# Attention and experts on one core: the experts' operands from split 32-bit floats to scaled pairs of 16-bit floats

## The chip, the cores and the metric

The kernel runs on one core of one Trainium2 chip. Its engines are PE (TensorE: matrix products, with weight loads listed as PEld), DVE (VectorE), ACT (ScalarE), POOL (GpSimd) and SP (SyncE, which here issues DMAs). Each works through its own queue in order. The metric is the device time of one execution in microseconds (us), the median of several runs.

## The reference

Attention with pooled queries for 8 batches of 8 heads, and then a mixture of 8 experts in which each token goes to one:

```python
q_pool = q.reshape(B, H, S // 2, 2, D).mean(axis=3)            # B=8 H=8 S=1152 D=64
scores = np.matmul(q_pool, k.transpose(0, 1, 3, 2)) / np.sqrt(D)
attn = softmax(scores)                                          # + 1e-9 in the sum
x = np.matmul(attn, v)  ->  rows of 512, N = 4608
logits = x @ w_gate
e_idx = np.argmax(logits, axis=1)
for e in range(8):
    h = np.maximum(x[mask] @ w1[e], 0.0)                        # w1: 512 x 1024
    ye = h @ w2[e]                                              # w2: 1024 x 512
    out[mask] = gate_w[mask, None] * eom[mask, e, None] * ye
```

## The kernel before

All products are exact to about 32-bit floats: a 32-bit operand is split into a high part that TensorE takes at speed and a low part with the rest, and a product is the sum of three: high by high, high by low, low by high.

**Attention** works on 32 pairs of heads, 18 steps each (one step is one head and 128 keys, 576 steps in all). In each step PE makes the scores of step s (two matmuls of 512 columns, L466), 1.5 products for row maxima two thirds of a pair ahead (L388, read by DVE at L389), and the product with v of the step six before (L495 to L497, 12 small matmuls a chunk, each with its weight load). ACT takes the exponential (L442), and for five of the 18 steps (PLP) a second one (L444) from which DVE subtracts; in the others POOL makes the low part (L450). The splitting of the next pairs' q, k and v is spread over the steps by tables (PREP0, PREPF, PREPE, PREP; three slots a step, counted from SLEAD steps before the start); their copies to the places where PE reads them are DMAs on SP. BURST says how many chunks of the product with v fall into which step. After each batch a router finds every token's expert, writes its row of x with its gate to the scratch tensor xrows (513 wide) and scatters its number into lists by expert.

**Experts** work on tiles of 256 tokens of one expert. Before attention ends, 256 tokens of the expert that leads by then are already gathered (tile -1); then come 18 dynamic tiles of 256 (two halves of 128) and 3 tiles of 128 ("one half", list 'S'). A tile's weights (4 MB) are loaded into raw1 and raw2, which are double, unless the expert is the same. For tile t, tile_ and head write out the order of PE, DVE and ACT by hand: layer one in four groups g (l1m makes the products into PSUM, l1e reads them out: ACT copies the half that comes from x's low part, DVE adds, ACT takes the relu, DVE the low part hl), with the split of w2 (split2) between them; then the split of the next tile's w1 (split1), layer two for the first 128 tokens (l2), the transposes of the next tile's x (xt: PE transposes, ACT copies the high part, DVE subtracts), layer two for the other half. y is scaled by the token's gate (xg column 512) and scattered to the output. A half tile's layer two uses plain 32-bit floats. The split parts are of type F32R: W1 and W2 exist once, x is double. A matmul of F32R brings its weight load with it. POOL has the gathers and scatters: after the last router 5 scatters, then the gathers of numbers (L839) and of rows (L850).

The products of layer one stand as follows, x holding its high part in columns 0 to w and its low part in w to 2w, W1[0] being the high part of w1:

```python
for c in range(4):
    for l in (0, 1) if c == 0 else (1, 0):
        n = w if l else 2 * w
        nc.tensor.matmul(hp[:, f, 0:n], lhsT=W1[l][g][:, c, fs], rhs=d['x'][:, c, 0:n], ...)
```

## Time and profile before

| | us |
|---|---|
| median of 3 runs | 1444.39 (1443.15 to 1447.83) |
| the profiled execution | 1445.07 |
| its span, first to last instruction | 1443.4 |
| PE busy | 1403.0 (97%) |
| DVE busy | 1095.0 (76%) |
| ACT busy | 976.2 (68%) |
| POOL busy | 1008.2 (70%) |

The trace comes from one execution, and its times are counted from the span's start. "Busy" is time in which at least one instruction of an engine runs; matmuls overlap, so PE's pace is read from the distance between the starts of successive matmuls, not from the length of one. [...] In the rows, five busy times stand in the order PE, PEld, DVE, ACT, POOL, each with its number of instructions; a tile name is the program's, `out<-in`, followed by shapes; a bracket at the end of a row is the time that the engine stood idle before it and what it waited for.

### The profile page before, as it was taken

What the parts mean: (1) busy time and instruction counts of PE and PEld (TensorE: products, weight loads), DVE (VectorE), ACT (ScalarE), POOL (GpSimd) and SP (SyncE); (2) the same over time, 40 slices, a digit from 0 to 9 for tenths busy, and PEclk for the clock granted to TensorE, in tenths of its full rate; (3) what the DMA queues carried; (4) which work ended last, traced back from release to release, by engine and by line L of the source; (5) the groups of instructions that cost most, each with busy time, mean ns of one, the idle gap of its engine ahead of it and who ended that gap; (6) DMA issues with size and microseconds to landing.
All of it is one profiled execution on the core that took longest, in us unless ns stands there. A gap on an engine that the chain in (4) does not pass through costs nothing. (4 is left out here: it accounts for less than half of the span.)

```text
span 1443.4 us, 40161 instructions
## 1 busy us (share of the span) xinstructions
PE 1403.0 (97%) x16056; PEld 1037.8 (72%) x16056; DVE 1095.0 (76%) x2404; ACT 976.2 (68%) x1769; POOL 1008.2 (70%) x1036
## 2 busy tenths in 40 slices
PE   7999999999999999999999999989999999999996
PEld 4566667666666666666666666778888888888874
DVE  6677878887887887787787887578787877778652
ACT  6687777777777877877776776746565655656542
POOL 6888999899899989989989998872323333323200
PEclk8999999999999999999999999999999999999999
DMA  4345344443553463354354432639546666363650
GB/s 155 106 131 157 114 122 131 132 122 99 141 145 89 124 166 94 96 164 125 88 145 117 138 116 62 234 106 360 173 154 232 222 235 232 122 219 98 230 188 8
DMA packets 92048, 212.57 MB, mean 147 GB/s; under 512 B 13357, under 2 KB 28925, under 8 KB 91855
## 3 DMA queue, kind: packets, MB, share of 16 engines
q1 hardware_dynamic: 81262, 188.35, 42.7%
q0 software_dynamic: 9152, 20.85, 4.2%
q8 instruction: 128, 2.10, 0.6%
q10 hardware_dynamic: 1440, 0.74, 0.2%
q14 instruction: 66, 0.53, 0.1%
HBM read 164.23 MB, written 23.02 MB: 130 GB/s over the span
## 5 line engine op out<-in xcount | busy, mean ns | idle before, releaser
L389 DVE TENSOR_REDUCE pm<-mp 128x1 f32<-128x384 f32 x864 | 447.5, 549 | 75.3 <-PE mp L388 68.9
L442 ACT ACTIVATE p<-sps 128x512 f32<-128x512 f32 x576 | 343.0, 596 | 207.6 <-PE sps L466 163.7
L450 POOL TENSOR_TENSOR pl<-p 128x512 f16<-128x512 f32 x414 | 423.2, 1040 | 61.2 <-ACT p L442 58.1
L388 PE MATMUL mp<-ka,qa 128*128 128x384 f16 x960 | 297.9, 327 | 3.0 <-DVE pm L389 2.4
L495 PE MATMUL av<-vt,p 128*128 128x65 f16 x2304 | 252.7, 193 | 0.3 <-DVE xb L514 0.3
L496 PE MATMUL av<-vt,p 128*128 128x64 f16 x2304 | 252.4, 194 | 0.0
L497 PE MATMUL av<-vt,pl 128*128 128x65 f16 x2304 | 252.2, 192 | 0.1
L388 PE MATMUL mp<-kb,qb 66*128 66x384 f16 x768 | 251.1, 327 | 0.0
L495 PEld LDWEIGHTS <-p 128*128 128x128 bf16 x2304 | 215.0, 97 | 27.1 <-DVE xb L514 1.0
L1021 PE MATMUL hps<-x,w1h 128*128 128x512 f32 (+1 forms) x704 | 228.7, 386 | 5.0 <-DVE x L1004 4.4
L496 PEld LDWEIGHTS <-p 128*128 128x128 bf16 x2304 | 213.2, 97 | 25.9 <-issue 0.2
L466 PE MATMUL sps<-qb,kb 69*128 69x512 f16 x576 | 219.4, 381 | 0.7 <-DMA qb<-mr 0.7
L466 PE MATMUL sps<-qa,ka 128*128 128x512 f16 x576 | 219.0, 380 | 0.0
L497 PEld LDWEIGHTS <-pl 128*128 128x128 f16 x2304 | 212.5, 98 | 0.3 <-POOL pl L450 0.3
L1021 PE MATMUL hps<-x,w1l 128*128 128x256 f32 (+1 forms) x704 | 164.7, 275 | 0.0
L1030 ACT COPY hs<-hps 128x512 f32<-128x512 f32 (+1 forms) x88 | 49.1, 558 | 170.4 <-PE hps L1021 162.6
L388 PEld LDWEIGHTS <-qa 128*128 128x128 f16 x960 | 94.4, 98 | 86.0 <-issue 1.3
L447 DVE TENSOR_TENSOR pl<-sps,p 128x512 f16<-128x512 f32 x162 | 111.2, 686 | 43.0 <-ACT sps L444 39.3
L1021 PEld LDWEIGHTS hps<-x,w1l 128*128 128x128 f32 x704 | 131.2, 189 | 12.9
L1021 PEld LDWEIGHTS hps<-x,w1h 128*128 128x128 f32 x704 | 121.8, 188 | 21.0 <-DVE x L1004 5.1
L839 POOL DMA_INDIRECT ids<-idscr,riD x36 | 43.8, 1215 | 131.7 <-DMA out_dram<-y,ids 121.0
L388 PEld LDWEIGHTS <-qb 66*128 66x128 f16 x768 | 75.3, 98 | 72.8 <-issue 8.4
(265 smaller groups left out, 3157.7 us busy)
## 6 DMA issues: line engine op xcount, KB each, us to landing
raw1b<-in_w_dram SPq DMA_DIRECT2D x24, 1024.0 KB
raw2b<-in_w_dram SPq DMA_DIRECT2D x24, 1024.0 KB
raw1a<-in_w_dram SPq DMA_DIRECT2D x22, 1024.0 KB
raw2a<-in_w_dram SPq DMA_DIRECT2D x22, 1024.0 KB
vp<-in_vL_dram SPq DMA_DIRECT2D x32, 576.0 KB
kpf<-in_kT_dram SPq DMA_DIRECT2D x31, 576.0 KB
qp<-in_qT_dram SPq DMA_DIRECT2D x31, 576.0 KB
ka<-xk SPq DMA_DIRECT2D x120, 144.0 KB
```

The costliest lines, as they stand in the source:

```text
L388: nc.tensor.matmul(mp, lhsT=l, rhs=r, start=j == 0, stop=j == len(ops) - 1)
L389: nc.vector.tensor_reduce(out=pm[:, i:i + 1], in_=mp, axis=AX.X, op=ALU.max)
L442: e_ = nc.scalar.activation(out=p32, in_=x, func=AF.Exp, scale=1.0 / 16)
L447: nc.vector.tensor_tensor(out=pl, in0=x, in1=ph, op=ALU.subtract)
L450: nc.gpsimd.tensor_tensor(out=pl, in0=p32, in1=ph, op=ALU.subtract)
L466: nc.tensor.matmul(x, lhsT=l, rhs=r, start=j == 0, stop=j == 1)
L495: nc.tensor.matmul(av_[:, qb, 0:65], lhsT=hi, rhs=vt[:, h, c, 0:65], start=c == 0 and qb == 0, stop=False)
L496: nc.tensor.matmul(av_[:, qb, 0:64], lhsT=hi, rhs=vt[:, h, c, 66:130], start=False, stop=False)
L497: nc.tensor.matmul(av_[:, qb, 0:65], lhsT=lo, rhs=vt[:, h, c, 0:65], start=False, stop=e and qb == 3 and h == 0)
L839: i = nc.gpsimd.indirect_dma_start(out=ids, out_offset=None, in_=self.idscr, in_offset=bass.IndirectOffsetOnAxis(ap=idx[:, j:j + 1], axis= ...
L1021: nc.tensor.matmul(hp[:, f, 0:n], lhsT=W1[l][g][:, c, fs], rhs=d['x'][:, c, 0:n], start=c == 0 and l == 0, stop=c == 3 and l == 0)
L1030: nc.scalar.copy(out=hs, in_=hp[:, :, w:2 * w])
```

## The change

Every operand of the experts becomes a pair of 16-bit floats (F16) instead of a pair of F32R. So that 16 bits hold them, weights and x are scaled by powers of two.

- *Scales of the weights.* During attention all 16 weight matrices are read once in 64 pieces of 512 KB (wst, on SP's queue), and ACT sums the magnitudes of each piece along its columns (wmag; from step 12 on, the loads six steps ahead of the sums, at steps 3, 11, 19, 23 and 35 of each 36). Near the end of attention wscale adds these over the rows (one matmul of 64 columns) and makes wt: for each expert one over the scale for w1 and w2, the scale of w1, and the product of both scales. pick takes a tile's expert out of wt with a one-hot product.
- *Scale of x.* rowscale takes each token's largest magnitude (DVE, over 512 columns), rounds it to a power of two, takes the reciprocal, lets ACT scale the gathered row in place, and puts what undoes all scales into gp, by which y is now scaled.
- *Splits.* cutw: ACT writes the high part, scaled, and DVE the low part in one pass. For tile -1's w1 ACT first scales in place, and POOL subtracts; its last w2 split goes from POOL to DVE.
- *Two sets* of split W1 and W2, one for tiles of either parity.
- *Layer one* is three products of w columns, each with its own weight load, into the same w columns; so nothing has to be added afterwards, and a group takes half the PSUM (three buffers instead of two). Relu and hl read PSUM.
- *Order.* xs (scl and rowscale for the next tile) stands after group 1; a half tile's next x is transposed ahead of layer two; in head xs stands ahead of split1, and two of the four split1 behind xt.
- y has 12 buffers instead of 4. The tables of attention (PREP, PREPE, BURST, PLP, TAIL, FWD, SLEAD) have new numbers; PREPE, PREP0 and PREPF are the same relative to the steps.

The rest of the experts (the part under tc.If) gets the same, and does not run with these inputs.

```diff
-FWD = 12
...
+FWD = 15
...
-BURST = {0: 1, 1: 2, 2: 1, 4: 1, 5: 1, 6: 1, 7: 2, 9: 1, 10: 1, 12: 1, 13: 2, 14: 1, 15: 3, 16: 1}
-PLP = (2, 8, 10, 11, 14)
+BURST = {0: 2, 1: 2, 4: 1, 5: 1, 6: 1, 7: 2, 10: 1, 11: 1, 12: 1, 13: 2, 14: 1, 15: 2, 16: 2}
+PLP = (3, 9, 10, 11, 13)
+WS0, WSP, WSL = 18, (3, 11, 19, 23, 35), 6
-TAIL = (10, 13, 15)
+TAIL = (10, 11, 15)
-SLEAD = 36
+SLEAD = 37
...
+        wm, wadd = moe.wmag(ld, lambda: sq.tile([128, S], F16, name="kjunk")), []
+        wsc = moe.wscale(psum, free)
...
+                if s >= WS0 - WSL and (s + WSL) % 36 in WSP:
+                    x = next(wm, None)
+                    if x is not None:
+                        wadd.append(x)
+                if wadd and s >= WS0 and s % 36 in WSP:
+                    wadd.pop(0)()
+                if WS0 + 36 * (64 // len(WSP) + 1) <= s < 18 * NP:
+                    next(wsc, None)
+                if moe.P1 and s == 18 * NP - 10:
+                    moe.rowscale(-1, 2, keep['px1'])
...
+                        nc.sync.dma_start(out=wst, in_=self.w1v[e, :, q])
...
+                    def add(wst=wst, i=i):
+                        nc.scalar.activation(out=junk()[:, 0:1024], in_=wst, func=AF.Abs, scale=2.0 ** -17, accum_out=self.keep['ws'][:, i:i + 1])
+                    yield add
...
+    def wscale(self, psum, free):
+        nc, k = self.tc.nc, self.keep
+        V, wt = nc.vector, k['wt']
+        g, gk = psum(True)
+        nc.tensor.matmul(g[:, 0:64], lhsT=k['ones'], rhs=k['ws'].bitcast(BF16)[:, 1::2], start=True, stop=True)
...
+        V.tensor_scalar(out=wt[:, 2:4].rearrange("p m e -> p (m e)"), in0=x, scalar1=2.0 ** -100, scalar2=2.0 ** 3, op0=ALU.max, op1=ALU.mult)
...
+        V.reciprocal(out=wt[:, 0:2], in_=wt[:, 2:4])
...
+    def pick(self, t, oh, s4, tm):
+        V, wt = self.tc.nc.vector, self.keep['wt']
+        V.tensor_tensor(out=tm, in0=wt, in1=oh.unsqueeze(1).broadcast_to([128, 4, 8]), op=ALU.mult)
+        V.tensor_reduce(out=s4, in_=tm, axis=AX.X, op=ALU.add)
+        self.T[t]['s'] = s4
+
+    def rowscale(self, t, h, px):
+        nc, d = self.tc.nc, self.T[t]
+        V = nc.vector
+        mx, sx, gp = px[:, 0:h], px[:, 2:2 + h], px[:, 4:4 + h]
+        for j in range(h):
+            V.tensor_reduce(out=mx[:, j:j + 1], in_=d['xg'][j][:, 0:512], axis=AX.X, op=ALU.max, apply_absolute_value=True)
+        V.tensor_scalar(out=mx.bitcast(U32), in0=mx.bitcast(U32), scalar1=0x7F800000, scalar2=None, op0=ALU.bitwise_and)
+        V.tensor_scalar(out=mx, in0=mx, scalar1=2.0 ** -100, scalar2=2.0, op0=ALU.max, op1=ALU.mult)
+        V.reciprocal(out=sx, in_=mx)
+        for j in range(h):
+            nc.scalar.activation(out=d['xg'][j][:, 0:512], in_=d['xg'][j][:, 0:512], func=AF.Copy, scale=sx[:, j:j + 1])
+            V.scalar_tensor_tensor(out=gp[:, j:j + 1], in0=d['xg'][j][:, 512:513], scalar=d['s'][:, h + 1:h + 2], in1=mx[:, j:j + 1], op0=ALU.mult, op1=ALU.mult)
+        d['gp'] = gp
...
-            ps_h = pool("ps_h", 2, space=PSUM)
+            ps_h = pool("ps_h", 3, space=PSUM)
...
-            W1 = [[wp1.tile([128, 4, 256], F32R, name=f"w1{x}{g}") for g in range(4)] for x in "hl"]
-            W2 = [p.tile([128, 8, 512], F32R, name=f"w2{x}") for x, p in (("h", wh), ("l", wq))]
-            X = [self.x0 if P1 else ma.tile([128, 4, 2 * TS], F32R, name="x0"), mb.tile([128, 4, 2 * TS], F32R, name="x1")]
+            W1_ = [[[p.tile([128, 4, 256], F16, name=f"w1{x}{g}{i}") for g in range(4)] for x in "hl"] for i, p in enumerate((wp1, wr))]
+            W2_ = [[p.tile([128, 8, 512], F16, name=f"w2{x}{i}") for x in "hl"] for i, p in enumerate((wh, wq))]
...
+            def xs(t):
+                if 'gp' not in T_[t]:
+                    scl(t)
+                    self.rowscale(t, halves(t), m1.tile([128, 6], F32, name="px", bufs=4))
+
+            def cutw(o, raw, sc, eng):
+                if eng is V:
+                    nc.scalar.activation(out=o[0], in_=raw, func=AF.Copy, scale=sc)
+                    V.scalar_tensor_tensor(out=o[1], in0=raw, scalar=sc, in1=o[0], op0=ALU.mult, op1=ALU.subtract)
+                    return
+                nc.scalar.activation(out=raw, in_=raw, func=AF.Copy, scale=sc)
+                nc.scalar.copy(out=o[0], in_=raw)
+                eng.tensor_tensor(out=o[1], in0=raw, in1=o[0], op=ALU.subtract)
+
             def split1(t, c, eng=V):
-                raw = raw1[(t + 1) % 2]
-                z = slice(256 * c, 256 * c + 256)
-                nc.scalar.copy(out=W1[0][c], in_=raw[:, :, z])
-                eng.tensor_tensor(out=W1[1][c], in0=raw[:, :, z], in1=W1[0][c].bitcast(F32), op=ALU.subtract)
+                W1 = W1_[(t + 1) % 2]
+                cutw([W1[0][c], W1[1][c]], raw1[(t + 1) % 2][:, :, 256 * c:256 * c + 256], T_[t]['s'][:, 0:1], eng)
 
             def split2(t, c, eng=V):
-                z = slice(2 * c, 2 * c + 2)
-                raw = raw2[(t + 1) % 2]
-                nc.scalar.copy(out=W2[0][:, z], in_=raw[:, z])
-                eng.tensor_tensor(out=W2[1][:, z], in0=raw[:, z], in1=W2[0].bitcast(F32)[:, z], op=ALU.subtract)
+                cutw([W[:, 2 * c:2 * c + 2] for W in W2_[(t + 1) % 2]], raw2[(t + 1) % 2][:, 2 * c:2 * c + 2], T_[t]['s'][:, 1:2], V)
...
-                        for l in (0, 1) if c == 0 else (1, 0):
-                            n = w if l else 2 * w
-                            nc.tensor.matmul(hp[:, f, 0:n], lhsT=W1[l][g][:, c, fs], rhs=d['x'][:, c, 0:n], start=c == 0 and l == 0, stop=c == 3 and l == 0)
+                        for i, (l, o) in enumerate(((0, 0), (0, w), (1, 0))):
+                            nc.tensor.matmul(hp[:, f, 0:w], lhsT=W1[l][g][:, c, fs], rhs=d['x'][:, c, o:o + w], start=f + c + i == 0, stop=f + c + i == 6)
...
-                hs = m1.tile([128, 2, TS], F32, name="hs", bufs=2)[:, :, 0:w]
-                nc.scalar.copy(out=hs, in_=hp[:, :, w:2 * w])
-                V.tensor_tensor(out=hs, in0=hp[:, :, 0:w], in1=hs, op=ALU.add)
+                hp = hp[:, :, 0:w]
 
                 def relu():
                     if halves(t) == 1:
-                        nc.scalar.activation(out=HR[:, z], in_=hs, func=AF.Relu)
+                        nc.scalar.activation(out=HR[:, z], in_=hp, func=AF.Relu)
                         return
-                    nc.scalar.activation(out=hh, in_=hs, func=AF.Relu)
-                    V.scalar_tensor_tensor(out=hl, in0=hs, scalar=0.0, in1=hh.bitcast(F32), op0=ALU.max, op1=ALU.subtract)
+                    nc.scalar.activation(out=hh, in_=hp, func=AF.Relu)
+                    V.scalar_tensor_tensor(out=hl, in0=hp, scalar=0.0, in1=hh, op0=ALU.max, op1=ALU.subtract)
...
+                xs(u)
                 for c in range(2):
                     split1(u, c)
                 pend.append(l2(t, 0))
                 gat(t + 3)
-                for c in range(2, 4):
-                    split1(u, c)
                 pend.pop(0)()
                 pend.append(l2(t, 1))
                 xt(u)
+                for c in range(2, 4):
+                    split1(u, c)
...
+                    if g == 1 and u is not None:
+                        xs(u)
...
+                if u is not None and halves(t) == 1:
+                    xt(u)
...
-                if u is not None:
+                if u is not None and halves(t) > 1:
```

**ACT in attention**, about steps 18 to 23 of a cycle of 36: p and sps are the exponentials, kpf, qs, xk and xq the scaled k and q and their high parts. Before:

```order
L442 ACTIVATE p_12329<-sps 128x512
L237 ACTIVATE kpf<-kpf,ik 128x576
L240 ACTIVATE qs<-qs,ik 128x576
L442 ACTIVATE p_12351<-sps 128x512
L237 ACTIVATE kpf<-kpf,ik 128x576
L442 ACTIVATE p_12379<-sps 128x512
L283 CAST xk_11982<-kpf 128x576
```

Now:

```order
L220 ACTIVATE kjunk,ak<-kpf 128x1152
L344 ACTIVATE vt_155<-vp,sc 128x9x64
L925 ACTIVATE kjunk,ws<-wst 128x1024
L443 ACTIVATE p_12332<-sps 128x512
...
L443 ACTIVATE p_12414<-sps 128x512
L238 ACTIVATE kpf<-kpf,ik 128x576 x2
L241 ACTIVATE qs<-qs,ik 128x576
L443 ACTIVATE p_12503<-sps 128x512
L284 CAST xk_12121<-kpf 128x576
L925 ACTIVATE kjunk,ws<-wst 128x1024
```

Two sums of weights stand around the scalings of k, and both scalings of k now follow each other.

**ACT where attention ends**: the last exponential, tile -1's w1, and xh, the high part of the x that the last router reads. Before:

```order
L442 ACTIVATE p_22228<-sps 128x512
L444 ACTIVATE sps<-sps 128x512
L984 CAST w1h_22601<-raw1a 128x1024
L984 CAST w1h_22602<-raw1a 128x1024
L566 CAST xh<-tp 128x256
L566 CAST xh<-tp 128x320
```

Now:

```order
L443 ACTIVATE p_22495<-sps 128x512
L445 ACTIVATE sps<-sps 128x512
L1076 CAST w1h_22883<-raw1a 128x1024
L1076 CAST w1h_22884<-raw1a 128x1024
L1075 ACTIVATE raw1a<-raw1a,s_93 128x4x256 x2
L1076 CAST w1h_22885<-raw1a 128x1024
L567 CAST xh<-tp 128x256
```

Three operations more stand between the last exponential and xh.

**DVE from tile -1 to tile 0**: hl ends layer one of tile -1, w1l is tile 0's w1, px and xg tile 0's rows, y and x as above. Before:

```order
L1038 SCALAR_TENSOR_TENSOR hl<-hs,hh 128x512
L985 TENSOR_TENSOR w1l_22605<-raw1b,w1h_22601 128x1024
L985 TENSOR_TENSOR w1l_22606<-raw1b,w1h_22602 128x1024
L985 TENSOR_TENSOR w1l_22607<-raw1b,w1h_22603 128x1024
L985 TENSOR_TENSOR w1l_22608<-raw1b,w1h_22604 128x1024
L1056 TENSOR_SCALAR y<-yp,xg 128x512
L1004 TENSOR_TENSOR x_22611<-xps,x_22611 128x4x128 x2
```

Now:

```order
L1129 SCALAR_TENSOR_TENSOR hl<-hps,hh 128x512
...
L960 TENSOR_REDUCE px<-xg 128x1 x2
L961 TENSOR_SCALAR px<-px 128x2
L962 TENSOR_SCALAR px<-px 128x2
L963 RECIPROCAL px<-px 128x2
L966 SCALAR_TENSOR_TENSOR px<-xg,s_23184,px 128x1 x2
L1073 SCALAR_TENSOR_TENSOR w1l_22895<-raw1b,s_23184,w1h_22891 128x1024
L1073 SCALAR_TENSOR_TENSOR w1l_22896<-raw1b,s_23184,w1h_22892 128x1024
L1148 TENSOR_SCALAR y<-yp,px_94 128x512
L1098 TENSOR_TENSOR x_22903<-xps,x_22903 128x4x128 x2
L1073 SCALAR_TENSOR_TENSOR w1l_22897<-raw1b,s_23184,w1h_22893 128x1024
L1073 SCALAR_TENSOR_TENSOR w1l_22898<-raw1b,s_23184,w1h_22894 128x1024
```

The maxima of tile 0's rows stand ahead of everything that splits its w1 and x.

## Rows read from the trace of the kernel before

**Rows 1.** Stages: stretch, length, busy us (x) by engine, PEclk, DMA, GB/s

```profile
102.00:930.00 828.00, 819.42 (x12270) 566.60 (x12269) 662.45 (x1742) 629.35 (x1241) 762.17 (x787) 1.00 0.46 128
942.06:970.23 28.17, 24.55 (x122) 19.57 (x122) 20.01 (x46) 13.04 (x18) 21.28 (x18) 1.00 0.34 85
970.23:994.67 24.44, 23.60 (x121) 19.62 (x121) 21.09 (x48) 13.46 (x19) 7.54 (x7) 1.00 1.01 380
...
1017.68:1363.29 345.61, 345.61 (x1802) 294.63 (x1800) 260.01 (x300) 198.30 (x270) 111.18 (x89) 1.00 0.54 191
...
1402.13:1418.47 16.34, 14.94 (x84) 10.83 (x85) 7.71 (x10) 7.51 (x13) 0.98 (x2) 1.00 0.19 70
```

**Rows 2.** Waits of PE from 50 to 942 us: total, times, longest

```profile
PE tp L328 <- DVE pm L389: 3.3, 7, 1.3
...
PE tp L579 <- ACT p L442: 0.2, 1, 0.2
```

**Rows 3.** Timeline of PE, one steady tile: start, length, engine, line, operation

```profile
1109.84 0.39 PE L1021 MATMUL hps<-x,w1h 128*128 128x512 f32 x1
...
1121.09 0.39 PE L1050 MATMUL yp<-w2h,hh 128*128 128x512 f32 x1
...
1122.00 0.39 PE L1051 MATMUL yp<-w2l,hh 128*128 128x512 f32 x1
```

**Rows 4.** Timeline of PE in attention; the last row a run of 32 fillers

```profile
403.68 0.38 PE L466 MATMUL sps<-qa,ka 128*128 128x512 f16 x1
...
404.11 0.33 PE L388 MATMUL mp<-ka,qa 128*128 128x384 f16 x1
...
404.77 0.19 PE L495 MATMUL av<-vt,p 128*128 128x65 f16 x1
404.80 0.19 PE L496 MATMUL av<-vt,p 128*128 128x64 f16 x1
...
940.06 1.95 PE L129 MATMUL idle<-ones 128*128 128x128 bf16 x32
```

**Rows 5.** Groups of instructions: count | busy us, mean ns | idle

```profile
L495 PEld LDWEIGHTS <-p 128*128 128x128 bf16 x2304 | 215.0, 97 | 27.1 <-DVE xb L514 1.0
...
L985 DVE TENSOR_TENSOR w1l<-raw1b,w1h 128x1024 fp32r<-128x1024 f32 x44 | 51.7, 1221 | 3.7 <-ACT w1h L984 3.7
```

**Rows 6.** Timeline of PE, layer two of a one-half tile and its successor

```profile
1409.60 7.03 PE L1048 MATMUL yp<-raw2a,hr 128*128 128x512 f32 x16
1416.47 0.60 PE L1001 MATMUL xps<-ident,xg 128*128 128x128 f32 x4
```

**Rows 7.** Hand-over: timelines of ACT, POOL, DMA issues (us to landing), PE

```profile
935.04 0.81 ACT L566 CAST xh<-tp 128x256 fp32r<-128x256 f32 x2 [0.39 <-PE tp L560]
...
944.23 1.07 POOL L677 DMA_INDIRECT idscr<-tid,posi  x1 [0.16 <-POOL w2l L991]
...
962.15 1.96 POOL L850 DMA_INDIRECT xg<-xrows,ids  x1 [0.30 <-issue]
...
xg<-xrows,ids POOLq DMA_INDIRECT x1, 4.8
...
967.63 1.04 PE L1001 MATMUL xps<-ident,xg 128*128 128x128 f32 x8
970.23 0.50 PE L1021 MATMUL hps<-x,w1h 128*128 128x512 f32 x1 [1.56 <-DVE x L1004]
```

**Rows 8.** Stretches early in attention, columns as in rows 1

```profile
50.00:52.00 2.00, 0.32 (x8) 0.31 (x9) 1.53 (x3) 0.95 (x2) 2.00 (x3) 1.00 0.39 88
52.00:54.00 2.00, 2.00 (x26) 1.35 (x23) 0.64 (x4) 0.15 (x1) 0.72 (x3) 0.51 0.61 138
54.00:56.00 2.00, 2.00 (x29) 1.43 (x28) 1.19 (x3) 0.83 (x2) 1.41 (x2) 0.64 0.62 146
```

**Rows 9.** Timeline of ACT: a sum of magnitudes over 1152 columns

```profile
318.81 1.15 ACT L219 ACTIVATE kjunk<-kpf 128x1152 f16<-128x1152 f32 x1
...
319.95 0.59 ACT L442 ACTIVATE p<-sps 128x512 f32<-128x512 f32 x1
```

More of the change, by code (lines that the diff above doesn't have):

```diff
@@ new lines, in wscale @@
+    def wscale(self, psum, free):
[3 more added lines that the diff above has]
+        nc.tensor.matmul(g[:, 0:64], lhsT=k['ones'], rhs=k['ws'].bitcast(BF16)[:, 1::2], start=True, stop=True)
+        x = g[:, 64:80]
+        V.tensor_reduce(out=x, in_=g[:, 0:64].rearrange("p (e q) -> p e q", q=4), axis=AX.X, op=ALU.add)
+        yield
+        V.tensor_scalar(out=x.bitcast(U32), in0=x.bitcast(U32), scalar1=0x7F800000, scalar2=None, op0=ALU.bitwise_and)
+        yield
+        V.tensor_scalar(out=wt[:, 2:4].rearrange("p m e -> p (m e)"), in0=x, scalar1=2.0 ** -100, scalar2=2.0 ** 3, op0=ALU.max, op1=ALU.mult)
+        free(gk)
+        yield
+        V.reciprocal(out=wt[:, 0:2], in_=wt[:, 2:4])
+        yield
+        V.tensor_tensor(out=wt[:, 3], in0=wt[:, 2], in1=wt[:, 3], op=ALU.mult)
+        yield
+        while -1 not in self.T:
+            yield
+        self.pick(-1, k['oh1'], k['s1'], k['tm1'])
@@ L1012, in l1m @@
                 d['hh'], d['hl'] = H
[L1013 removed]
+                W1 = W1_[(t + 1) % 2]
+                hp = ps_h.tile([128, 2, TS], F32, name="hps")
                 w = 128 * halves(t)
@@ L1321, in body @@
         pairs = [(b, hp) for b in range(nb) for hp in range(4)]
-        attention(tc, qT, kT, vL, wg, keep, xrows, idscr, cum, pairs, m.setup, m.scat, init, m.exps, m.turn if m.P1 else None)
+        attention(tc, qT, kT, vL, wg, keep, xrows, idscr, cum, pairs, m.setup, m.scat, init, m.exps, m)
         m.run()
```

51 lines of the change are left out of this document (39 added, 12 removed).

## The prediction

> **What bounds the kernel now.** I read the stages first, then the waits of TensorE, then single matmuls. The stage table [rows 1] shows two long stages. In attention (102 to 930 us) PE is busy 819 of 828 us. In the expert stage the 15 steady tiles between 1017.68 and 1363.29 us have PE busy all 345.61 us, 23.04 us a tile, while DVE works 260.0 (17.3 a tile), ACT 198.3 and POOL 111.2. The waits of PE in attention are small: 3.3 us in 7 waits is the largest, and ACT's exponentials hold it up once, for 0.2 us [rows 2]. So PE's own pace is the time in both stages, and a change pays by what it takes from PE's stream, or costs by what it makes PE wait.
>
> In a steady tile layer one takes PE 11.25 us (1109.84 to 1121.09), layer two and the transposes the other 11.79; matmuls of 512 columns in split 32-bit floats start (1122.00-1121.09)/4 = 0.2275 us apart [rows 3]. In attention two matmuls of 512 columns in 16-bit floats take 0.43 us, 0.215 each, and four of 384 take 0.66, 0.165 each; the 65-column ones start 0.03 us apart, each with a weight load of its own of 97 ns [rows 4, 5]. The first expert tile is not steady: 28.17 us, with PE busy 24.55, and the second takes 24.44 [rows 1].
>
> **The change part by part.**
>
> *Layers one and two of the 18 two-half dynamic tiles.* The sum of columns stays: 32 times 512 + 256 becomes 32 times 3 x 256. At 256 columns no 16-bit matmul stands in the trace. In proportion to the 384s it would start every 0.1075 us or a little more, on the line through 512 and 384 every 0.115; I take 0.111, between them. Layer one: 96 x 0.111 = 10.66, against 11.25, so -0.59 (bounds -0.93 and -0.21). Layer two: 48 x (0.2275 - 0.215) = -0.60; with 0.22 for a 512, which single rows show as often, -0.36. Together I take -1.15 a tile, for the 17 steady ones (994 to 1386 us): **-19.5** (bounds -26 and -9.7).
>
> That PE stays the bound there follows from DVE: 17.3 us, less four passes over 512 columns (the old sum of two halves, each about half of the 1.22 us of a 1024-column pass [rows 5], so -2.4), plus two maxima over 512 (1.2), some nine small operations of 0.2 us: 17.9 of 21.9 us. ACT loses four copies and gains two scalings. The second set of split weights takes away waits that are not there in steady tiles, so I cost it at nothing; what covers it is the full PE.
>
> *The three one-half tiles.* Layer one takes 1409.60 - 1402.13 = 7.47 us [rows 1, 6]; 32 filler matmuls of 128 columns in 16 bits, each with its weight load, take 1.95 us, at most 0.061 each, about 0.057 without the last one's drain [rows 4]. 96 x 0.057 = 5.5: three times -2.0. The next tile's transposes now stand before layer two, so PE no longer waits for x behind it: 2.0 us stood from 1416.47 to 1418.47 [rows 1, 6], of which four transposes need some 0.4; -1.6 twice. The weights that must be split meanwhile need 4 x 1.22 = 4.9 us of DVE, under 1416.47 - 1409.60 = 6.87 of PE. Sum **-9.2**. [...]
>
> *The first expert tile and its hand-over.* Here the change costs. On ACT two in-place scalings now stand ahead of the last two casts of the router's x (in the order above): after the last exponential, whose end I read at 930.7, come five operations of about 1.03 us, to 935.9, where xh started at 935.04 [rows 7]: the router and all behind it +0.9. On POOL the last split is gone for which the scatters waited until 944.23 [rows 7]; they now wait for the router alone: about 1.1 us earlier, and so is every gather behind. The second gather of the next tile's rows was issued at 962.15 and landed 4.8 us later, 966.95 [rows 7]; now about 965.9. Before, nothing but PE's transposes waited for it, at 967.63. Now DVE stands at the second maximum of those rows, and queued behind it are the split of w1, y and x's low part; ACT stands at the scaling of xg, and behind it are w1's casts and x's. From 965.9: maximum 0.65, three small ones 0.6, two scalings on ACT 1.1, to 968.3; two casts of w1 2.0, two of x 1.1; on DVE w1l to 971.8, y 0.7, two passes of x 1.3: layer one of the next tile starts at about 973.8, against 970.23 [rows 7]: **+3.6**, the 0.9 included. PE would have done its layers by 964.8 (942.9, layers of 10.7 and 10.3, and some 0.9 of waiting for hidden units to be read out). [...] The second tile, 24.44 us with its own small waits, keeps about 1.3 of those and comes to 23.3: **-1.1**. Sum +4.2 (bounds 0 and 9).
>
> *Attention.* 64 sums of magnitudes on ACT: one over 1152 columns holds ACT from 318.81 to 319.95, 1.14 us with its read-out [rows 9], so 1.02 each for 1024, 65 us over some 727 us. ACT is busy 629 of 828 us [rows 1], so it goes to about 85%; five come in 36 steps of 1.55 us. Adding up ACT's work step by step in the new order, I find it behind by at most some 2.4 us, after the two that fall close to the scalings of k. PE asks for a step's weights 6 steps later, so most is hidden. Queued behind ACT's insertions are the next exponential, POOL's subtraction (762 of 828 us busy, no room to catch up) and DVE's. 33.5 MB more are read at a DMA share of 0.46; on SP a load stands ahead of k's and q's copies, whose issue was shifted by the new tables. One small matmul is added. I take **+1.5** (bounds -2, if the new tables save some of the waits of rows 2, and +10).
>
> Sum: -19.5 - 9.2 + 4.2 + 1.5 = -23.0. From the profiled execution's 1445.07 (span 1443.4 and 1.7 around it) this gives 1422.1; that execution is 0.7 above the median of the runs, so **1421.4**.
>
> **Rivals.**
>
> *ACT becomes attention's bound (slower).* Place: every insertion, where ACT, then DVE or POOL, come late to PE. Price: if the whole 1.02 us of each reaches PE, 65 us, and the run is near 1485. It decides from (23.0 + 1.5)/64 = 0.38 us an insertion on. For: POOL is full, and DVE waits for ACT's second exponential in 5 of 18 steps. Against: PE waited 0.2 us for ACT in all of attention [rows 2], and ACT had a quarter of its time free. 0.08; 1446 to 1485.
>
> *16 bits are no faster per column here.* If layers one and two keep their 23.04, the third weight load eating what the format gives, -19.5 falls away: about 1441. Against are 0.215 and 0.165 [rows 4]. 0.08.
>
> *DVE becomes the bound in steady tiles.* The chain of maxima, reciprocal and scaling stands in line with DVE's splits, and y waits for PE. If a tile comes to 22.6, 17 x 0.7 is lost of the gain: 1433. 0.08.
>
> *The gathers land early or PE keeps its clock:* 4 us better, 1417. 0.03.
>
> *Weight loads in line.* If no 16-bit weight load is hidden behind a matmul of the same rows, each of 144 matmuls pays 97 ns: 14 us a tile, some 250 us in all, near 1680. The 0.03 us between attention's matmuls, each with its 97 ns load, speak against it [rows 4, 5]: 0.01. [...]
>
> **How the numbers follow.** My forecast has 0.72: steady tiles -9.7 to -26, the hand-over 0 to 9, attention -2 to 10; not all at their ends together, 1409 to 1437. With the rivals at 1417 and 1433 inside it the range 1409 to 1437 holds 0.8. A difference under 0.3% (4.3 us) cannot be told from none. Faster than 1440.1: the forecast 0.72, 1433 and 1417 together 0.11, and a little under half of the 1441 case 0.03: 0.86. The rest of that case, and the best end of the ACT case, is no change: 0.06. Slower: 0.08.
>
> **What would show it.** Steady tiles of 21.9 us with PE still full, 512-column matmuls 0.215 apart and 256-column ones 0.11: part one. Layer one of the one-half tiles at 5.5 us and no wait for x: part two. Between the first and second expert tile two gaps of PE, of some 3.5 and 4.7 us, ended by the scaled xg and by x's low part, and then a granted clock near 0.5: part three. Attention's PE busy within 2 us of before, with waits for ACT still short: part four. I am wrong if PE waits for exponentials or DVE in attention add up to over 10 us, or if steady tiles show gaps.

## The result, and the profile after

The changed kernel takes 1424.17 us, median of 4 runs (1422.08 to 1426.78), against 1446.11 (1443.15 to 1448.0) for the kernel before in the same session: a ratio of 0.9851, 95% interval 0.9825 to 0.9877. It is faster by 22 us (1.5%); 1421.4 was forecast, with a range of 1409 to 1437. Its profiled execution took 1423.65 us (span 1421.9) against 1445.07 (1443.4), 21.4 less.

The stages of the changed kernel, columns as in [rows 1], where PEclk is the share of its full clock that PE was granted: attention; the last pair of heads alone; tiles -1 and 0; the 17 steady tiles; 15 of them; the first one-half tile.

```profile
102.00:930.00 828.00, 818.28 (x12254) 569.84 (x12251) 666.23 (x1755) 690.70 (x1360) 762.02 (x787) 1.00 0.55 164
...
910.84:932.16 21.32, 18.81 (x347) 13.83 (x346) 11.28 (x28) 17.73 (x35) 15.12 (x17) 1.00 1.02 391
950.76:977.75 26.99, 22.45 (x153) 14.84 (x153) 15.64 (x45) 9.91 (x14) 18.72 (x19) 1.00 0.36 99
977.75:1005.07 27.32, 24.26 (x153) 15.96 (x153) 25.59 (x60) 16.88 (x20) 7.96 (x6) 0.88 0.93 348
1005.07:1373.76 368.69, 368.69 (x2582) 254.49 (x2581) 291.14 (x439) 213.90 (x268) 119.62 (x96) 1.00 0.58 207
1026.78:1352.48 325.70, 325.70 (x2282) 224.92 (x2280) 258.70 (x390) 191.44 (x240) 111.55 (x88) 1.00 0.57 203
...
1386.43:1399.10 12.67, 12.67 (x117) 8.76 (x116) 8.01 (x14) 6.89 (x10) 0.97 (x1) 1.00 0.39 137
```

PE is still the bound: busy all of 325.70 us, 21.71 a tile where [rows 1] had 23.04, with DVE at 17.2 of it. ACT has 61 us more in attention, and PE is as busy as before. Tile 0, 24.44 long before, is longer, at a granted clock of 0.88. The account goes by the starts of PE's work in both profiled executions. Its first mark is a group of 12 fillers, products of ones that nothing reads, which PE makes behind attention's last product. Of the kernel before, besides [rows 1]: the last pair of heads alone, the 17 steady tiles, and the fillers in the timeline of PE.

```profile
909.94:929.09 19.15, 18.85 (x359) 14.06 (x358) 9.45 (x21) 15.32 (x31) 14.82 (x16) 1.00 1.02 400
994.67:1385.86 391.19, 391.19 (x2037) 333.44 (x2036) 292.82 (x338) 223.20 (x304) 120.81 (x97) 1.00 0.56 198
...
933.48 0.84 PE L129 MATMUL idle<-ones 128*128 128x128 bf16 x12
```

| stage | before | after | difference | forecast |
|---|---|---|---|---|
| attention, to the 12 fillers behind its last product | 933.48 | 936.89 | +3.4 | +1.5 |
| from there to tile 1 | 61.19 | 68.18 | +7.0 | +4.2 |
| 17 steady tiles | 391.19 | 368.69 | -22.5 | -19.5 |
| three one-half tiles | 47.11 | 37.79 | -9.3 | -9.2 |

Single matmuls of the changed kernel, timeline of PE: the start, the length, and how many such rows are taken together.

```profile
1026.78 0.38 PE L1114 MATMUL hps<-x,w1h 128*128 128x256 f16 x2
...
1037.26 0.38 PE L1142 MATMUL yp<-w2h,hh 128*128 128x512 f16 x1
...
1042.44 1.04 PE L1095 MATMUL xps<-ident,xg 128*128 128x128 f32 x8
...
1386.43 0.28 PE L1114 MATMUL hps<-x,w1h 128*128 128x128 f16 x2
...
1391.79 0.61 PE L1095 MATMUL xps<-ident,xg 128*128 128x128 f32 x4
```

Layer one of a steady tile is 1037.26 - 1026.78 = 10.48 us, 0.1092 for a product of 256 columns; 24 products of 512 columns take 1042.44 - 1037.26 = 5.18 (0.2158), against 0.2275 in [rows 3]. In the one-half tile layer one takes 1391.79 - 1386.43 = 5.36, 0.0558 for 128 columns; the next x's four transposes follow it, and layer two stands behind them.

The hand-over after attention: PE with ACT and DVE in the router, then with the waits in brackets at tile 0's start. The fillers of 128 columns show the clock.

```profile
936.89 0.84 PE L130 MATMUL idle<-ones 128*128 128x128 bf16 x12
...
939.41 0.82 ACT L567 CAST xh<-tp 128x256 fp32r<-128x256 f32 x2
...
939.95 0.38 PE L580 MATMUL tp<-xh,wgt 128*128 128x256 f32 x1 [1.16 <-ACT xh L567]
...
942.55 3.38 PE L130 MATMUL idle<-ones 128*128 128x128 bf16 x30
...
942.65 0.24 DVE L611 COPY lg<-tp 128x80 f32<-128x80 f32 x1 [0.61 <-PE tp L605]
942.84 2.39 DVE L1073 SCALAR_TENSOR_TENSOR w2l<-raw2a,s,w2h 128x1024 f16<-128x1024 f32 x1
...
945.15 0.23 DVE L612 TENSOR_TENSOR tp<-lg,tp 128x80 f32<-128x80 f32 x1
...
947.12 3.58 PE L130 MATMUL idle<-ones 128*128 128x128 bf16 x32
...
949.78 1.07 POOL L678 DMA_INDIRECT idscr<-tid,posi  x1 [5.63 <-DVE cum L673]
...
971.80 0.69 DVE L960 TENSOR_REDUCE px<-xg 128x1 f32<-128x512 f32 x1 [1.02 <-DMA xg<-xrows,ids]
...
974.11 1.27 PE L1095 MATMUL xps<-ident,xg 128*128 128x128 f32 x8 [1.47 <-ACT xg L965]
...
977.75 0.27 PE L1114 MATMUL hps<-x,w1h 128*128 128x256 f16 x1 [2.37 <-ACT x L1097]
...
980.20 0.37 PE L1114 MATMUL hps<-x,w1h 128*128 128x256 f16 x1 [2.18 <-DVE x L1098]
```

The router's xh starts 2.52 us after the 12 fillers (935.04 - 933.48 = 1.56 before, [rows 7]): +0.96. Between DVE's copy of the logits and the sum that waits on it stands a piece of w2's split, 2.39 us long. The next fillers take 3.38 and 3.58 us where 32 took 1.95 in [rows 4], at a granted clock of 0.50 from 942 to 950. Three waits, for the scaled rows and both parts of x, open tile 0. The clock in both places, columns as above:

```profile
938.00:940.00 2.00, 0.84 (x7) 0.70 (x7) 0.23 (x2) 2.00 (x5) 2.00 (x2) 1.00 0.00 0
940.00:942.00 2.00, 1.84 (x6) 1.13 (x6) 1.60 (x4) 2.00 (x3) 2.00 (x1) 0.60 0.00 0
942.00:944.00 2.00, 1.91 (x17) 1.84 (x18) 1.39 (x3) 0.21 (x1) 2.00 (x2) 0.50 0.00 0
...
976.00:980.00 4.00, 0.27 (x1) 0.10 (x1) 4.00 (x5) 4.00 (x6) 3.39 (x3) 0.74 0.94 375
980.00:984.00 4.00, 3.80 (x19) 2.61 (x19) 4.00 (x5) 1.87 (x2) 3.39 (x3) 0.50 1.01 349
984.00:988.00 4.00, 4.00 (x35) 3.45 (x34) 3.76 (x17) 0.60 (x1) 1.10 (x2) 0.90 1.03 391
```

### The profile page after: what moved, and what is told of

It is laid out like the page before. It is cut to its first block, busy times and chain, and to the rows that moved or that the text cites. A ratio compares the mean times of both kernels' runs of the same rounds, so it can differ in the third digit from the quotient of the medians.

```text
span 1421.9 us, 41747 instructions
## 1 busy us (share of the span) xinstructions
PE 1376.4 (97%) x16761; PEld 952.1 (67%) x16761; DVE 1099.0 (77%) x2535; ACT 1034.2 (73%) x1854; POOL 1004.5 (71%) x1035
## 3 DMA queue, kind: packets, MB, share of 16 engines
q8 instruction: 133, 2.18, 0.6%
## 5 line engine op out<-in xcount | busy, mean ns | idle before, releaser
L1114 PE MATMUL hps<-x,w1h 128*128 128x256 f16 (+1 forms) x1408 | 218.9, 267 | 5.3 <-ACT x L1097 2.4
L1114 PE MATMUL hps<-x,w1l 128*128 128x256 f16 (+1 forms) x704 | 183.0, 267 | 0.0
L1114 PEld LDWEIGHTS <-w1h 128*128 128x128 f16 x1408 | 134.5, 98 | 23.2 <-issue 3.3
L868 POOL DMA_INDIRECT xg<-xrows,ids x41 | 47.8, 1167 | 103.1 <-ACT hh L1128 46.8
L1149 POOL DMA_INDIRECT out_dram<-y,ids x41 | 54.9, 1339 | 92.2 <-DVE y L1148 56.0
```

What stands on the lines that cost most here:

```text
L868: self.lastg = nc.gpsimd.indirect_dma_start(out=xg, out_offset=None, in_=self.xrows[0:rows], in_offset=bass.IndirectOffsetOnAxis(ap=self.T ...
L1114: nc.tensor.matmul(hp[:, f, 0:w], lhsT=W1[l][g][:, c, fs], rhs=d['x'][:, c, o:o + w], start=f + c + i == 0, stop=f + c + i == 6)
L1149: nc.gpsimd.indirect_dma_start(out=self.out, out_offset=bass.IndirectOffsetOnAxis(ap=d['ids'][j][:, 0:1], axis=0), in_=yt, in_offset=None, ...
```

## The experiments

All are edits of the changed kernel. Those timed once are read by their traces; a ratio is against the kernel before.

**1. The hand-over, w2's split.** The last split of tile -1's w2 goes behind the router on DVE:

```diff
                 totals1()
-                split2(t, 3, nc.gpsimd)
                 totals2()
...
                 acts.pop(0)()
+                split2(t, 3)
                 loads(t + 2, behind=z['lg'])
```

> The changed kernel with the last split of tile -1's w2 moved on ACT and DVE behind the other three, so that it no longer stands between the copy of the logits and their sum in the last router. Theory A (this split is what holds the router, 2.39 us): from the end of attention's last matmul to the first scatter 2.2 us less, layer one of tile -1 starts 2.2 us earlier in the same count, or about 3.9 if PE's clock also recovers, and tile 1 starts at about 1002 to 1003 instead of 1005.1. Rival B (the scatters wait for POOL's own splits, which end at 944.1, or the gathers are bound elsewhere): under 0.7 us of it reaches tile 1.

1418.82 us in its run. Now the sum follows the copy, and the first scatter stands 1.9 us nearer to the fillers, by this timeline of DVE and POOL:

```profile
939.69 0.24 DVE L611 COPY lg<-tp 128x80 f32<-128x80 f32 x1 [0.46 <-PE tp L605]
939.96 0.24 DVE L612 TENSOR_TENSOR tp<-lg,tp 128x80 f32<-128x80 f32 x1
...
945.37 1.08 POOL L678 DMA_INDIRECT idscr<-tid,posi  x1 [3.72 <-DVE cum L673]
```

From the 12 fillers to tile -1 are 10.61 us (13.87 in the changed kernel), to tile 1 65.75 (68.18). By these two executions the split's place is 2.4 of the 7.0. Each is a single one. In three others with the split between copy and sum and the rest of the hand-over as it was (experiments 5, 10 and 11) tile 1 starts 67.50 to 68.44 after the fillers, so 1.8 to 2.7 is what can be told. That the split holds up the scatters is clear: the first one stands 12.86 to 12.90 after the fillers in all six executions with the split in this place, and 9.22 to 10.99 in the four where it is not in the router (experiments 1, 3, 7 and 12). In experiments 4, 6 and 9 it stands at another step of the router, and the first scatter at 12.18 to 12.96. The clock still fell here (0.50 from 940 to 942). Over the 14 us from the fillers on 0.88 was granted, against 0.63 in the changed kernel's execution. With the split in place and the same 0.88 (experiment 5) tile 1 starts at 67.82, so the difference is not the clock's alone.

**2. The hand-over, the order at tile 0.** w1's first two splits stand ahead of the maxima of tile 0's rows:

```diff
-                xs(u)
+                scl(u)
                 for c in range(2):
                     split1(u, c)
                 pend.append(l2(t, 0))
+                xs(u)
```

> The changed kernel with two of the four splits of tile 0's w1 ahead of the maxima and the scaling of tile 0's rows instead of behind them. Theory A (the queues of ACT and DVE behind the late gather are the hand-over): full layer one of tile 0, which started at 980.2, starts 2.2 to 2.6 us earlier against the second gather's landing, and tile 1 at about 1002.6. Rival B (y or the clock is the bound there): under 1 us, tile 1 after 1004.

1425.2 us, and tile 1 starts 71.51 after the fillers, later than without the edit. The timeline of PE and ACT has the reason in this execution:

```profile
972.80 1.27 PE L1095 MATMUL xps<-ident,xg 128*128 128x128 f32 x8 [1.49 <-ACT xg L965]
...
976.37 0.59 ACT L1097 CAST x<-xps 128x512 f16<-128x512 f32 x1 [3.01 <-remote]
...
979.93 0.59 ACT L1097 CAST x<-xps 128x512 f16<-128x512 f32 x1 [2.98 <-remote]
```

The transposes run from 972.80 to 974.07, but ACT, idle for 3 us each time, starts its two copies only at 976.37 and 979.93. I saw the like in the executions of experiments 8 and 9, in part of 6, and not in those of the changed kernel and of experiments 1 and 3. What holds the signal was not found; of the order alone this run says nothing.

**3. Both edits together.**

> Both edits of the hand-over together: tile -1's last w2 split behind the other three, and two splits of tile 0's w1 ahead of the maxima of tile 0's rows. Theory A (the late start of tile 0 with the w1 edit alone was an odd completion of PE's transposes, 3 us late twice, and not a rule): layer one of tile 0 runs in full within 6.2 us of the second maximum's start, against 8.2 us with the w2 edit alone, and the median falls to about 1416 to 1418. Rival B (the transposes are finished late again, because PE stands still behind them with nothing else in its queue): tile 0 in full 9 us or more after that maximum, median 1421 or above.

1419.58 us (4 runs, 1418.8 to 1421.73), ratio 0.980 (0.9776 to 0.9824). Timeline of DVE and PE where tile 0 begins:

```profile
970.47 0.69 DVE L960 TENSOR_REDUCE px<-xg 128x1 f32<-128x512 f32 x1 [1.26 <-DMA xg<-xrows,ids]
...
975.48 0.27 PE L1114 MATMUL hps<-x,w1h 128*128 128x256 f16 x1 [0.46 <-issue]
```

From the second maximum's start to layer one in full are 975.48 - 970.47 = 5.01 us (4.85 in experiment 12), against 980.20 - 971.80 = 8.40 in the changed kernel and 8.12 to 8.28 in experiments 1, 4 to 7, 10 and 11. Tile 1 starts 62.28 after the fillers, 5.9 sooner and 1.1 from the 61.19 before. So what was queued on ACT and DVE behind the late rows is 3.4 of these 5.9. Another 3.1 came ahead of the rows, from the split's place and the clock together, and 0.6 went again behind them. The clock stayed at 1.00 through the router, though PE was as little busy in one stretch (0.85 of 940 to 942) as in the changed kernel (0.84 of 938 to 940): what decides there is left open. This version is faster than the kernel before, and its four runs all lie below the changed kernel's four (1422.08 to 1426.78), which were timed in another session.

**4. Attention, the scaling of tile -1's rows 20 steps earlier.**

```diff
-                if moe.P1 and s == 18 * NP - 10:
+                if moe.P1 and s == 18 * NP - 30:
```

> The changed kernel with the maxima and the scaling of tile -1's rows 20 steps earlier in attention (its rows were there since 813 us). Theory A (this scaling, ahead of an exponential on ACT and of PE's transposes, is the loss of the last eight steps): PE's wait of 1.4 us for the scaled rows goes, and the last scores start 1.3 to 2 us earlier, at 930.2 to 930.9. Rival B (ACT is the bound in the last steps anyway, the wait turns into one for exponentials): last scores after 931.6.

1426.78 us. PE no longer waits for the scaled rows, but once 5.0 us for DVE; timeline of DVE and POOL there:

```profile
894.64 4.55 DVE L966 SCALAR_TENSOR_TENSOR px<-xg,s,px 128x1 f32<-128x1 f32 x1
895.13 4.03 POOL L451 TENSOR_TENSOR pl<-p 128x512 f16<-128x512 f32 x4
```

A product of one element per partition, elsewhere 0.2 us, stands on DVE while POOL makes four subtractions in a row, and ends with them. The last scores start at 936.76, so theory A has its wait right and the time wrong, and rival B has the time by another cause. The last pair itself takes 20.13 us here instead of 21.32: the scaling did cost there, but this earlier place costs more.

**5. Attention without the sums.** The loop of wmag goes, and the scale is a constant:

```diff
-                    def add(wst=wst, i=i):
-                        nc.scalar.activation(out=junk()[:, 0:1024], in_=wst, func=AF.Abs, ...)
-                    yield add
+        return
+        yield
```

> The changed kernel without the 64 sums of magnitudes on ACT and without their 64 loads (33.5 MB); the scales come from a constant instead. It leaves out that part of the computation. Theory A (the sums are hidden behind PE): ACT's busy time in attention falls by about 65 us, the first scores of the last pair start within 1 us of 910.8, and the expert stage is unchanged. Theory B (my +1.5 us, the sums push PE): the last pair starts at 909.3 or earlier. Theory C (ACT's insertions cost what the new tables save): the last pair starts 3 us or more earlier, under 908.

1421.72 us. In the stage row of attention ACT has 54 us less than in the changed kernel, and PE the same 818 us:

```profile
102.00:930.00 828.00, 818.43 (x12252) 569.78 (x12249) 665.52 (x1758) 636.43 (x1242) 761.01 (x786) 1.00 0.44 128
```

The last pair starts at 908.81, where executions with the same attention as the changed kernel start it between 907.27 and 912.81. The sums and their 33.5 MB cost nothing that stands out of that spread. It is 5.5 us wide, and this is one execution, so the bounds of 1 to 3 us in the expectation could not be told apart: a cost of 1.5 us, as forecast, is neither shown nor excluded.

**6. Attention without the scaling of tile -1's rows.**

```diff
-                    moe.rowscale(-1, 2, keep['px1'])
+                    nc.vector.memset(keep['px1'], 1.0)
...
```

> The changed kernel without the maxima and without the scaling of tile -1's rows in attention's last steps (their scale is put at one, so this tile's x stays unscaled; two small products of DVE stay). From the first to the last scores of the last pair of heads it was 19.15 us before and 21.3 us in all runs of the changed attention. Theory A (the row scaling, 1.34 us of ACT ahead of an exponential behind 1.9 us of DVE, makes most of that): 19.4 to 19.9 us, and PE's wait of 1.4 us for the scaled rows is gone. Theory B (the new tables of attention, or the scalings of raw1a among the last exponentials, make it): 20.8 us or more.

1419.37 us. The last pair, same columns as above, took 21.32 us in the changed kernel and 19.15 before; here

```profile
909.03:928.95 19.92, 18.62 (x347) 13.76 (x346) 9.68 (x24) 17.48 (x34) 15.14 (x17) 1.00 1.03 397
```

In the nine executions with this attention left as it is the last pair takes 21.31 to 21.33, so the difference is clear of that spread. The scaling is 1.4 of the 2.2 us by which the last pair grew, the length of PE's one wait there for ACT's xg (1.4). Experiments 7 and 12, in whose last pair no w1 of tile -1 is scaled in place, have it at 20.95: some 0.4. The rest is open.

**7. One set of split weights.**

```diff
-            W1_ = [[[p.tile([128, 4, 256], F16, name=f"w1{x}{g}{i}") ...] for i, p in enumerate((wp1, wr))]
+            W1_ = [[[p.tile([128, 4, 256], F16, name=f"w1{x}{g}") ...] for p in (wp1,)] * 2
```

and W2_ likewise.

> The changed kernel with one set of split W1 and W2 for both parities of tiles instead of two. Theory A (PE is full and the splits' order already waits for layer one and two, so the second set hides waits that are not there): a steady tile stays at 21.7 us, the median within 4 us of 1424. Rival B (w2's splits wait for layer two of the tile before, and layer two for them): steady tiles of 22.5 us or more, 14 us or more in all.

1430.1 us (4 runs), ratio 0.9866 (0.9842 to 0.989). Fifteen steady tiles:

```profile
1032.92:1358.62 325.70, 325.70 (x2281) 224.91 (x2280) 258.60 (x390) 194.67 (x240) 109.64 (x85) 1.00 0.57 201
```

They take what they take with two sets, to 0.01 us. The 6 us that it loses are in the hand-over: PE waits 6.3 us for POOL's w1l of tile -1, since raw1a landed only at 943, where the changed kernel had scaled it at 929. Its load was issued at 935.4 instead of 909.0, after this wait of SP (waits: total, times, longest):

```profile
SPq L1036 <- PE av L505: 17.0, 1, 17.0
```

So the load stood behind attention's last products with v. That the buffers now share memory with a tile of attention would explain it, but was not tried.

**8. 16 bits in the old form.** 512 + 256 columns and the sum of columns, as before, in 16-bit floats:

```diff
-                        for i, (l, o) in enumerate(((0, 0), (0, w), (1, 0))):
+                        for l in (0, 1) if c == 0 else (1, 0):
+                            n = w if l else 2 * w
...
-                hp = hp[:, :, 0:w]
+                nc.scalar.copy(out=hs, in_=hp[:, :, w:2 * w])
+                V.tensor_tensor(out=hs, in0=hp[:, :, 0:w], in1=hs, op=ALU.add)
```

> The changed kernel in 16 bits, but with layer one in the form of before: products of 512 and 256 columns into both halves, copied by ACT and added by DVE, two PSUM buffers. Theory A (the gain of steady tiles is the format's, not the form's): layer one 32 x (0.2158 + 0.1092) = 10.4 us as against 10.48, a steady tile 21.6 to 21.8, the median within 5 us of 1424, with DVE at about 20 us a tile instead of 17.2. Rival B (DVE with copies and sums again becomes the bound): steady tiles of 22.2 us or more, 8 us or more in all.

1491.66 us (4 runs), ratio 1.0309 (1.0276 to 1.0342): slower than before. Layer one takes 10.40, but PE has gaps. One tile, columns as in the stages:

```profile
1034.60:1059.66 25.06, 22.65 (x121) 11.37 (x120) 19.62 (x30) 15.04 (x20) 7.61 (x7) 1.00 0.60 216
```

and the timeline of ACT in it:

```profile
1044.01 1.33 ACT L965 ACTIVATE xg<-xg,px 128x512 f32<-128x512 f32 x2 [3.38 <-DVE px L963]
```

No engine is full: DVE is busy 19.6 of 25.06. ACT stands 3.4 us for the rows' maxima, and behind it the chain of copy, addition, relu and low part runs late into layer two, whose first half takes 8.6 to 8.8 us instead of 5.18 while PE waits for hh and hl. Another order of these queues was not tried.

**9. The new form in 32 bits.** Layer one as three products of 256 in F32R; layer two stays 16-bit:

```diff
-            W1_ = [[[p.tile([128, 4, 256], F16, name=f"w1{x}{g}{i}") ...] for i, p in enumerate((wp1, wr))]
+            W1_ = [[[wp1.tile([128, 4, 256], F32R, name=f"w1{x}{g}") ...] for x in "hl"]] * 2
```

> The changed kernel with layer one's operands (w1 and x) in split 32-bit floats, one set of W1, and three products of 256 columns each; layer two stays in 16 bits. Theory A (columns alone count): 96 x 0.114 = 10.9 us for layer one, a steady tile 22.2, the median about 8 us above 1424. Theory B (the pitch of 0.1167 us that 32-bit matmuls of 256 and 128 columns had before is a floor of the weight load): 11.2 us, a tile 22.45, about 13 us above. Theory C (the 188 ns that such a weight load takes are a floor): 18 us, a tile 29.3, 130 us above.

1452.22 us (10 runs), ratio 1.0026 (1.0014 to 1.0038). A steady tile and a one-half tile:

```profile
1005.56:1028.12 22.56, 22.56 (x154) 16.98 (x153) 18.13 (x27) 12.88 (x16) 6.60 (x6) 1.00 0.69 243
1389.38:1407.17 17.79, 17.79 (x118) 14.18 (x117) 7.68 (x14) 6.89 (x10) 0.97 (x1) 1.00 0.33 122
```

and the pitch in layer one, timeline of PE:

```profile
1028.66 0.40 PE L1114 MATMUL hps<-x,w1h 128*128 128x256 f32 x2
...
1029.02 0.40 PE L1114 MATMUL hps<-x,w1h 128*128 128x256 f32 x2
```

PE is full, with 0.12 for 256 columns (1029.02 - 1028.66 = 0.36 for three). Layer one comes to an estimated 11.4 us, a steady tile of 22.6 less the 21.71 - 10.48 = 11.23 that the rest of one takes in the changed kernel; 128 columns come to an estimated 0.109 in the one-half tile here ((17.79 - 12.67 + 5.36) / 96) and 0.112 over the three ((53.94 - 37.79 + 3 x 5.36) / 288), hardly less. The weight load of F32R is 190 ns long, that of 16 bits 98; whether it makes this pitch is not shown. The 17 steady tiles, mostly 22.45 and 22.76 in turn, lose 383.82 - 368.69 = 15 us to the changed kernel and the one-half tiles 53.94 - 37.79 = 16, which the expectation left out. With experiment 8: in this kernel neither the old form in 16 bits nor the new form of layer one in 32 bits is faster than before. What PE's own stream gains in layer one comes with the format (10.40 in the old form, 10.48 in the new); the new form spares the copy and the sum for which PE waited in experiment 8.

**10. POOL beside DVE's splits.** 36 multiplications on POOL in layer one of tiles 6 to 9, three a group, which read hh:

```diff
+                            for _ in range(3):
+                                nc.gpsimd.tensor_tensor(out=HR[:, 0:4]..., in0=HR[:, 4:8]..., in1=H[0][:, 2 * g - 2:2 * g]..., op=ALU.mult)
```

> The changed kernel with added work on POOL that nothing needs: nine multiplications of 512 elements during layer one of each of tiles 6 to 9. It asks why the w2 split that was moved to DVE took 2.39 us beside POOL's splits, and two products of one element 4.68 us beside POOL's subtractions with the scaling moved 20 steps. Theory A (an operation of DVE with two sources in SBUF stands until POOL's running operations end): in those tiles the w2 and w1 splits that meet POOL's work take 1.5 us or more on the mean and up to 4 us, those that read PSUM (hl, x, y) keep their 0.68 to 0.75. Theory B (no such wait): all durations within 5% of the other tiles' 1.27 and 0.68 us, and tiles of 21.7 us.

1457.42 us. Groups of instructions of one shape, in ns the least, median and most, then the stretch: the split of w2 in the tiles ahead of these and in them, the low part of the hidden units, and POOL's own.

```profile
L1073 DVE SCALAR_TENSOR_TENSOR w2l<-raw2b,s,w2h x4: 1277/1279/1284, 1113.1 to 1125.8; 128x1024 f16<-128x1024 f32 x4
L1073 DVE SCALAR_TENSOR_TENSOR w2l<-raw2b,s,w2h x8: 1277/1571/2920, 1160.7 to 1241.6; 128x1024 f16<-128x1024 f32 x8
...
L1129 DVE SCALAR_TENSOR_TENSOR hl<-hps,hh x15: 677/691/692, 1140.2 to 1244.9; 128x512 f16<-128x512 f32 x15
...
L1334 POOL TENSOR_TENSOR hr<-hr,hh x36: 1151/1167/2029, 1132.8 to 1242.2; 128x512 f32<-128x512 f32 x36
```

The split, both of whose sources are in SBUF, takes up to 2.92 us for 1.28; hl, one of whose sources is in PSUM, stays at 0.69, and two maxima in a row keep their 1.27 (from 1173.42, POOL's work from 1173.92). Away from POOL's work the split keeps its 1.28 in the same tiles. So the like of the hand-over's 2.39 us can be made at will. The four tiles take 26.4 to 31.2 us, because PE waits for hh and hl, and that makes the run's time. Theory A has both right, the split (2.92) and hl (0.69); what makes the split stand is not shown beyond these forms. In experiment 4 a DVE product stood 4.55 us, through four POOL instructions and not one.

**11. The next x behind layer two in the one-half tiles, as before.**

```diff
-                if u is not None and halves(t) == 1:
-                    xt(u)
...
-                if u is not None and halves(t) > 1:
+                if u is not None:
                     xt(u)
```

> The changed kernel with the next tile's transposes behind layer two of the one-half tiles, as they were before. Theory A (the new order alone takes away PE's wait for x): the wait of about 1.6 us comes back twice, one-half tiles with a successor of 14.2 us instead of 12.67. Rival B (w1's splits are as late as x): under 0.5 us each.

1423.51 us. The first one-half tile, 12.67 in the changed kernel:

```profile
1370.46:1384.07 13.61, 12.88 (x117) 8.83 (x116) 8.12 (x15) 6.88 (x10) 2.04 (x3) 1.00 0.60 216
```

PE waits for x again, 1.4 us for ACT and 1.0 for DVE; the second tile takes 14.22, and the three together 40.95, 3.2 more, as the forecast's two waits of 1.6 had it (2.4 of them stand as waits in the profile). The time of the whole run does not show it: its 12 fillers started 3.6 us sooner than in the changed kernel's execution.

**12. On top of experiment 3:** two of tile -1's w1 splits on DVE, the other two behind the router's xh, and the 16-bit layer two in the first and the last one-half tile (which leaves the scale of w2 out of their y).

```diff
+            def h16(t):
+                return halves(t) == 2 or t in (nd, NU - 1)
...
-                with tc.issue_after(self.exps[WSTEP[c]]):
-                    split1(order[0], c, nc.gpsimd)
+                with tc.issue_after(self.exps[-3 if c < 2 else -1]):
+                    split1(order[0], c, V if c < 2 else nc.gpsimd)
```

> Built from what the runs showed: the two edits of the hand-over; of tile -1's w1 two splits on DVE (one operation of ACT instead of two) and the other two behind the router's x; and layer two of the first and the last one-half tile in pairs of 16-bit floats, their w2 split in the tile before. Theory A (ACT's six operations ahead of the router's x, and the 32-bit layer two of 6.87 us, are what is left): the router's x 1 us and the last scores 0.8 us earlier, two one-half tiles 1.7 us shorter, a median of 1413 to 1416. Rival B (DVE or ACT becomes the bound of the one-half tiles, and tile -1 waits for its last splits): no more than 1 us better than both edits alone, 1418 to 1420.

1418.72 us (5 runs, 1413.18 to 1421.17), ratio 0.9793 (0.9766 to 0.9821): not to be told from experiment 3. The first and the last one-half tile gain 0.7 us in all, of 3.4 expected, because PE then waits, above all 1.6 us for hl.

## Why the prediction was right, point by point

**The sum.** -23.0 was forecast from the profiled execution, -21.4 came. Two terms missed in opposite directions, the steady tiles 3.0 better and the hand-over and attention 4.7 worse. That the sum came out 1.6 us from the forecast is luck to that extent.

**Steady tiles, -19.5 against -22.5.** The mechanism held, and the term was sized too small. Layer one came to 0.1092 for 256 columns, between the proportional 0.1075 and the 0.111 taken, so -0.77 a tile for -0.59; layer two to 0.2158 for 512, so 48 x 0.0117 = -0.56. Together -1.33, 17 times -22.6. The line through 512 and 384 was the poorer of the two estimates for 256. (The 0.1075 is half of a 512; in proportion to the 384s, as the forecast calls it, 256 columns come to 0.110.) DVE was put at 17.9 a tile and measures 17.2, so the rival of a DVE bound had no ground. Two sets of weights cost and bring nothing in steady tiles (experiment 7), as taken.

**The one-half tiles, -9.2 against -9.3.** Layer one, forecast at 5.5, takes 5.36; the moved transposes are worth 3.2 (experiment 11).

**Attention, +1.5 against +3.4.** Eight executions with this attention start the last scores between 928.60 and 934.14, median 930.8, which is +1.7 on the 929.09 of the one execution before; the profiled one lies 1.4 above that. ACT was put at 85% and is at 83%. That the sums do not make ACT the bound is shown (experiment 5); whether they cost a microsecond or two is not. The step that is shown to cost was not among those named: the scaling of tile -1's rows holds up PE for 1.4 us (experiment 6).

**The hand-over, +4.2 against +7.0: here a step failed.** +0.9 for the router's xh came as +0.96. The next step said that POOL, rid of the last split, would scatter 1.1 us earlier; the first scatter came at 949.78 - 936.89 = 12.89 us behind the fillers, where before it was 944.23 - 933.48 = 10.75: 2.1 later. The split had not vanished. It had moved to DVE, and there into the router's own chain, between two steps of 0.24 us, and beside POOL it took 2.39 us. I had followed the queue that it left and not the queue that it joined. Undone, it returns 2.4 us, 1.8 to 2.7 with the spread (experiment 1). The rows of the next tile came late with it: the second maximum starts 971.80 - 936.89 = 34.91 us behind the fillers, for a forecast of 965.9 - 933.48 = 32.4, and these 2.5 are most of the 2.8 that the part missed. The clock also fell in the router, with the split there (0.50 from 942 to 950) and without (experiment 1, 0.50 from 940 to 942), which I had not foreseen. The rest of the part held: from the second maximum to layer one in full 8.40 us for a forecast of 7.9, the stands of PE (1.5 us for the scaled rows and 2.37 + 2.18 for x, where 3.5 and 4.7 were named), the fall of the clock behind them (0.50 from 980 to 984), and the place, the queues of ACT and DVE behind the late rows (experiment 3: 5.01). Only tile 0 did not get shorter: 27.32, not 23.3, since the second wait and the slow clock fall into it and not into tile -1. The +4.2 has 1.7 in it for a fall of PE's clock behind its stands, an estimate that no run shows by itself: in [rows 8] 0.51 and 0.64 were granted in the two stretches of 2 us behind one in which PE was busy 0.32, so 2 x 0.49 + 2 x 0.36 = 1.7 us of full clock were missing. In the changed kernel 0.50 and 0.90 were granted in the two stretches of 4 us from 980 on, of which PE was busy 3.80 and 4.00: by the same count an estimated 3.80 x 0.50 + 4.00 x 0.10 = 2.3.

**The rivals.** ACT did not become the bound (experiment 5). 16 bits are faster per column (0.2158 for 512, against 0.2275), and no load stands in line with its matmul: each load is 98 ns long, and the matmuls start 0.1092 apart at 256 columns and 0.0558 at 128. The case that PE keeps its clock did not occur (0.50 from 980 to 984).

## What to carry to other kernels

Count what a form of product costs at its own width and in its own format: here three 16-bit products of 256 columns took PE about as long as two of 512 and 256 (10.48 and 10.40 us in layer one) and left nothing to be added, and the same three in 32 bits took more than the two (an estimated 11.4, and 11.25). When a step is moved from one engine to another, follow it into the new queue and look between which two short steps of a chain it lands, and who reads SBUF beside it (a split of 1.28 us took up to 2.92 beside POOL's work, experiment 10). A step that waits for a late transfer belongs behind the work that does not need that transfer.
